# Transposes with the whole array, moved fill matmuls and a new instruction order in a gated-linear-attention and mixer kernel

## The chip, the cores and the metric

The kernel runs on one core of a Trainium2 chip. The metric is the device time of one execution in microseconds (us): the median of several runs. A profile of one more execution gives the trace that is quoted here; its span is a little shorter than the timed runs, since it runs from the first to the last instruction.

## What is computed

First a recurrence over 768 steps for 4 batches and 8 heads of width 48, then a two-layer mixer over tokens and one over channels.

```python
for t in range(S):                                   # S = 768
    state = alpha[:, :, t, :, None] * state + einsum('bhd,bhe->bhde', k[:, :, t], v[:, :, t])
    y[:, :, t] = einsum('bhd,bhde->bhe', q[:, :, t], state)
x = y as [batch 4, token 768, channel 384]
h = maximum(x.T @ w_tok1, 0) @ w_tok2                # 768 -> 256 -> 768, over tokens
u = x + h.T
out = u + maximum(u @ w_ch1, 0) @ w_ch2              # 384 -> 1536 -> 384, over channels
```

## The kernel before

**Attention by blocks.** Each batch is cut into three blocks of 256 steps, so there are twelve blocks, numbered n = 0 to 11. A block's q, k, v and alpha come in four loads (`ld_qt`, `ld_kt`, `ld_vt`, `ld_at`) of 384 KB in float32. In SBUF, partition p holds steps 2p and 2p+1, which the code calls the two values of s (or `sl`); the two halves of the partitions (`hf`) are the two chunks of 128 steps of a block. The steps for one block are:

- `ln`, `cum`: the logarithm of alpha (ACT) and its running sum by matmuls with a triangular matrix; for blocks 0 to 2 (`WIDE`) in the form `lnw`, `cumw`, which spends more TensorE and fewer element-wise passes. `E` and `IE` are the exponentials of plus and minus that sum (ACT).
- `qq`, `kk`: q times E and k times IE, packed in bfloat16 with 64 columns a head (`pkq`, `pkk`); on DVE or POOL. The other blocks have `P`, `k0a` and `q0r` before them. `vb` is v in bfloat16.
- `trq`, `trk`: transposes of `pkq` and `pkk` on TensorE into PSUM; `evq`, `evk`: their copies to SBUF (`tpq`, `tpk`), on ACT or DVE.
- `G0`, `G1`: products of keys and queries; `mask0`, `mask1`: DVE multiplies them by the causal mask and writes `gtm`.
- `K`: the new state's part; `s`, `sa`, `sm`: the state carried on by DVE and POOL.
- `y` (from `gtm` and `vb`), `ia`, a small read called `fe`, `ib` (the inter-chunk part from the state): all in one pair of PSUM banks. `x0`, `x1`: its two halves copied to bfloat16.

**Mixer by batches.** `t1` (tokens 768 to 256) with its relu copies `ht`; `t2` back to 768, added to x in `u`; transposes `up` with copies `ut`; `c1` (24 groups of three matmuls of 384 columns each) with relu copies `rt`; `c2` (six outputs of twelve matmuls), added in `o` and stored by `st`. For batch 0 the matmuls of `t1` are twelve operations of their own, so that each can start when its block's x is there.

**Order.** Nothing is scheduled at run time: `ORDER` is a list of names, each with the letter of its engine (t TensorE, s ACT, v DVE, g POOL, y the load queue on SP), found beforehand by a search. Every engine works through its own names in that order. `Plan.decode` walks the list with a cost model and a due time for every operation; what it decides in the program that runs is which buffer, which PSUM bank or pair of banks each value gets. The transfers of the weights (`ldw_wt1`, `ldw_wt2`, three pieces `ldw_wc1`, two pieces `ldw_wc2`) are issued by POOL, each after the landing of the last load that stands before it in the list. Instructions of DVE and POOL[...] (`kk`, `qq`, `vb`, `sm`, `P`, `k0a`, `q0r`) wait for one another in list order where they change engines.

**Fills.** Before some TensorE steps of blocks 0 to 2 stand three optional operations f0, f1 and f2, which multiply zeros into the bank that the step will overwrite. Those with the letter t are issued, those with n are not. Their purpose is that TensorE keeps busy while its inputs are not there. In the order before, 56 such matmuls of 192 columns are issued, 24 of them ahead of everything else.

**Array modes.** `tr` (64-row transposes), `y`, `ia` and `ib` use the array cut by rows (mode "R" in the planner), `G` and `K` cut by rows and columns ("G"), and all else the whole array. The planner counts 95 ns for a change of mode.

Of the kernel before, what the change touches and what calls it, by code (L numbers as in the profile page):

```python
# [9 lines left out]
BF16 = mybir.dt.bfloat16  # L10
# [53 lines left out]
class Plan:  # L64
# [51 lines left out]
    def decode(self):  # L116
# [14 lines left out]
        for o in self.order:  # L131
# [45 lines left out]
            if e == "PE":  # L177
                a, b = st, st + occ
                while True:
                    w1 = (wi + 1) * 3413.0  # L180
                    if a < w1:
                        d = min(b, w1) - a
                        acc += d
                        a += d
                    if b < w1:
                        break
                    warm = acc > 3000.0 or (warm and acc > 1750.0)
                    wi, acc = wi + 1, 0.0
            if o.dma is not None:
# [6 lines left out]
                else:  # L196
                    s = max(st + lead, dma_in)
                    dma_in = self.landed(s, dur * (1.0 if s < 16000.0 else LATER))
                    o.end = dma_in + tail
# [26 lines left out]
LATER = 1.06  # L226
B, H, S, D = 4, 8, 768, 48
# [10 lines left out]
WIDE = (0, 1, 2)  # L238

# [3 lines left out]
def build(g):  # L243
# [8 lines left out]
    def attention(n):  # L252
# [5 lines left out]
        def O(name, eng, i, **kw):  # L258
            return P.op(f"{name}{n}", eng, pr(i), **kw)

        def fill(nm, bank, sizes=(4, 6, 8)):
            if n >= NB:
                return []
            return [O(f"f{j}{nm}_", {"PE": pe([192] * z)["PE"], "NONE": (0.0, 0.0)}, -100, writes=[bank],
                      emit=lambda e, z=z: g.fill(bank, z)) for j, z in enumerate(sizes)]
# [17 lines left out]
        else:  # L283
# [21 lines left out]
        bk, bq, tpk, tpq = V("pair"), V("pair"), V("tpk"), V("tpq")  # L305
        trk = O("trk", pe([64] * 8), 8, writes=[bk], reads=[pkk], preds=[kk] + fill("trk", bk), emit=lambda e: g.tr(bk, pkk, 2, 1), mode="R")
        trq = O("trq", pe([64] * 8), 8, writes=[bq], reads=[pkq], preds=[qq] + fill("trq", bq), emit=lambda e: g.tr(bq, pkq, 1, 4), mode="R")
        evk = O("evk", either(dve(1024, True), act(1024)), 9, writes=[tpk], reads=[bk], preds=[trk],
                emit=lambda e: g.trev(e, tpk, bk))
        evq = O("evq", either(dve(1024), act(1024)), 9, writes=[tpq], reads=[bq], preds=[trq],  # L310
                emit=lambda e: g.trevq(e, tpq, bq))
        gtm = V("gtm")
        masks = []
        for sl in range(2):
            gp = V("pair")
            G = O(f"G{sl}_", pe([128] * 4), 10 + sl, writes=[gp], reads=[tpk, tpq], preds=[evk, evq] + fill(f"G{sl}", gp),
                  emit=lambda e, sl=sl, gp=gp: g.gmm(gp, tpk, tpq, sl), mode="G")
# [8 lines left out]
        for hf in range(nst):  # L326
# [4 lines left out]
            else:  # L331
# [11 lines left out]
               emit=lambda e: g.inter(yp, tpq, [st and st[0] for st in states[:2]], 0), mode="R")  # L343
        fe = O("fe", either(act(4), dve(4)), 15, reads=[yp], preds=[ia], emit=lambda e: g.fence(e, yp))
        io = O("ib", pe([48] * 4), 15, writes=[yp], reads=[tpq] + [v for v, _ in use], preds=[fe],
               emit=lambda e: g.inter(yp, tpq, [st and st[0] for st in states[:2]], 1), mode="R")
# [104 lines left out]
f1cumw_0n ld_at0y ln0s f2G0_0n f0G0_1n f0y_2n f2trk_0n f2cumw_1t f2trk_1n f0trk_1n f1trk_1n f2G1_0t ld_at1y ln1s  # L451
f2trq_0t f2K_0n f0y_1n f0cumw_0n f2cumw_0n cumw0t E0s IE0s f0G0_2n f0trk_0n f2G1_1n f0cumw_2n f0trk_2n f1cumw_2n
f0K_0n f2G0_1n ld_qt0y qq0v f0cumw_1t f1y_0n f1K_0n f1cumw_1n f1G1_2n cumw1t f2trq_2n f0G1_0t f0y_0n f0trq_0n
f1K_2n f1trq_0n Et0s ld_kt0y f2trq_1n f0K_2n f1trk_0n ld_qt1y f1G1_0n f0trq_1n kk0v f1trq_1n E1s trq0t ld_vt0y
Et1s evq0s ld_kt1y f2y_0n qq1v trk0t trq1t ld_at2y evk0v G1_0t f2G0_2n f2cumw_2n f0G1_2n vb0v ld_vt1y K0t s0_0v
IE1s kk1g evq1s f0G0_0t f2K_2n ld_qt2y mask1_0v f1G0_0t G0_0t trk1t ln2s f0G1_1n cumw2t sa1_0v sm1_0v f1G1_1n
vb1g evk1s f0trq_2n f1G0_1n mask0_0v G0_1t f2y_2n mask0_1v G1_1t y0t ia0t f2y_1n E2s qq2g mask1_1v f0K_1n f1y_2n
IE2s Et2s fe0s ib0t f2K_1n x0_0s x1_0s f1trq_2n ldw_wt10g f1y_1n f2G1_2n f1K_1n K1t f2trk_2t f1trk_2n trq2t
evq2s ld_kt2y kk2v y1t sa0_1v sm0_1g ld_vt2y trk2t evk2v ld_at3y ln13s sa1_1v P3g r13s vb2s G1_2t lnP3s ia1t
mask1_2v ld_qt3y fe1s ldw_wt20g f1G0_2t G0_2t mask0_2v K2t sm1_1g sa0_2v cum3t q0r3g IE3s ib1t x1_1s sm0_2v y2t  # L460
ia2t t1_0_1_0t t1_0_1_1t fe2v ib2t E3s qq3v ld_kt3y t1_0_0_0t k0a3v kk3v x0_1s t1_0_1_2t t1_0_1_3t t1_0_0_1t
x0_2s t1_0_0_2t t1_0_0_3t t1_0_0_4t x1_2s t1_0_0_5t t1_0_1_4t t1_0_1_5t ldw_wc10g trq3t ht_0_0s trk3t evk3v
ht_0_1s t2_0_3t t2_0_1t t2_0_2t t2_0_0t t2_0_4t t2_0_5t u_0_3v u_0_1v u_0_2v ldw_wc12g evq3s G1_3t u_0_0v u_0_4v
u_0_5v ld_at4y P4g lnP4s up_0_1t ut_0_1s up_0_0t G0_3t cum4t E4s ut_0_0v up_0_2t ut_0_2v mask1_3v c1_0_3_0t
rt_0_3_0s ln14s IE4s ldw_wc11g ld_qt4y r14s c1_0_2_0t rt_0_2_0v c1_0_3_1t rt_0_3_1s c1_0_0_0t c1_0_1_1t
rt_0_0_0s ld_at5y q0r4v qq4g P5g ld_vt3y c1_0_2_1t rt_0_2_1s c1_0_9_0t c1_0_8_1t c1_0_1_0t rt_0_1_0s c1_0_10_0t
rt_0_10_0s rt_0_1_1s c1_0_11_1t ldw_wc20g rt_0_11_1v c1_0_11_0t rt_0_11_0s c1_0_9_1t rt_0_9_1s rt_0_9_0s
rt_0_8_1v c1_0_4_0t mask0_3v c1_0_6_1t trq4t evq4s ldw_wc21g lnP5s vb3v rt_0_4_0v c1_0_10_1t c1_0_5_0t rt_0_5_0s
K3t s0_3v sa1_3v rt_0_6_1s c1_0_5_1t rt_0_5_1s ld_kt4y c1_0_4_1t k0a4g kk4v ld_kt5y ln15s cum5t rt_0_10_1s r15s
sm1_3g c1_0_7_0t IE5s y3t ia3t trk4t rt_0_7_0v c1_0_0_1t c1_0_7_1t rt_0_4_1s fe3v ib3t evk4v G0_4t rt_0_0_1s  # L470
G1_4t k0a5g kk5g rt_0_7_1s x1_3v c1_0_6_0t mask0_4v mask1_4v rt_0_6_0v x0_3s c1_0_8_0t ld_qt5y c2_0_2_0t
c2_0_1_0t ld_vt4y E5s rt_0_8_0s c2_0_4_0t c2_0_2_1t c2_0_4_1t c2_0_5_0t c2_0_5_1t q0r5g trk5t qq5v trq5t ld_vt5y
c2_0_1_1t c2_0_5_2t c2_0_1_2t evk5v ld_at6y vb4v K4t sa0_4v sm0_4g evq5s G1_5t mask1_5v ld_kt6y c2_0_4_2t sa1_4v
c2_0_4_3t o_0_4v c2_0_2_2t G0_5t sm1_4v vb5s K5t sa0_5v c2_0_1_3t mask0_5v c2_0_0_0t c2_0_5_3t y4t ia4t fe4v y5t
ld_at7y P6g sm0_5g ia5t ld_qt6y fe5v ib4t x0_4s c2_0_2_3t ib5t x1_4s o_0_1v x0_5v ld_at8y st_0_4y ld_qt7y x1_5v
ld_vt6y P7g lnP7s c2_0_0_1t c2_0_0_2t cum7t ln16s k0a6v ln17s ld_vt9y t1_1_0t r17s r16s lnP6s ld_kt7y st_0_1y
t1_1_1t ht_1_1s o_0_5v ld_vt8y q0r6g ht_1_0v c2_0_3_0t c2_0_0_3t t2_1_1t ld_vt7y st_0_5y t2_1_2t t2_1_0t t2_1_3t
o_0_0v E7s P8g cum6t IE6s IE7s c2_0_3_1t ld_qt9y ln18s u_1_1v t2_1_4t q0r7g qq7g vb6g u_1_0v up_1_0t t2_1_5t
u_1_2v u_1_3v u_1_4v up_1_1t c2_0_3_2t c2_0_3_3t ut_1_0s ut_1_1v c1_1_6_0t rt_1_6_0s c1_1_4_0t u_1_5v c1_1_9_0t
rt_1_9_0s k0a7g up_1_2t ut_1_2s ld_at9y c1_1_0_0t kk7v o_0_2v kk6v rt_1_4_0v c1_1_10_0t rt_1_10_0v E6s c1_1_8_0t  # L480
c1_1_9_1t rt_1_9_1v c1_1_1_0t rt_1_1_0v c1_1_0_1t trk7t evk7v rt_1_8_0s rt_1_0_0s trq7t trk6t evk6v lnP8s
rt_1_0_1s c1_1_6_1t rt_1_6_1v ld_kt8y ld_kt10y evq7s o_0_3v c1_1_11_0t rt_1_11_0v ln19s c1_1_3_0t rt_1_3_0s qq6g
trq6t evq6s K6t s0_6v vb7g K7t cum8t P9g sa1_6v c1_1_2_0t rt_1_2_0v ld_qt8y k0a8g sm1_6g c1_1_7_1t ld_at11y
ld_at10y st_0_2y r18s c1_1_8_1t c1_1_7_0t sa0_7v sm0_7v sa1_7v sm1_7v lnP9s rt_1_7_1v IE8s c1_1_10_1t c1_1_5_0t
rt_1_5_0v E8s G1_6t rt_1_8_1s rt_1_7_0s rt_1_10_1s G0_6t kk8g mask0_6v G0_7t mask0_7v c1_1_5_1t ld_qt11y
ld_vt11y vb8g c2_1_0_0t c2_1_0_1t c2_1_0_2t c1_1_3_1t rt_1_3_1s c1_1_1_1t c2_1_0_3t P10g rt_1_1_1s lnP10s
mask1_6v q0r8g qq8g ln110s G1_7t rt_1_5_1v mask1_7v st_0_0y ld_vt10y K8t sa0_8v cum9t IE9s P11g E9s c2_1_1_0t
c2_1_1_1t c2_1_1_2t y6t ia6t trq8t o_1_0v st_1_0y trk8t r19s fe6s ib6t c1_1_2_1t evk8v x1_6v c2_1_1_3t q0r9v
o_1_1v evq8s c1_1_4_1t G1_8t sm0_8v x0_6s G0_8t c2_1_2_0t c2_1_2_1t qq9g mask1_8v c1_1_11_1t ln111s lnP11s
c2_1_2_2t c2_1_2_3t rt_1_2_1s rt_1_4_1v r111s c2_1_4_0t c2_1_4_1t st_0_3y ld_kt11y mask0_8v y8t ld_kt9y ld_qt10y  # L490
ia8t fe8s rt_1_11_1v y7t ia7t k0a11v trq9t fe7v ib8t ib7t x1_7s c2_1_4_2t c2_1_4_3t x0_7v cum11t vb9g x1_8v
x0_8s t1_2_1t t1_2_0t ht_2_1s c2_1_3_0t c2_1_3_1t o_1_2v ht_2_0s q0r11g st_1_1y t2_2_2t o_1_4v evq9v u_2_2v
t2_2_3t u_2_3v k0a9g E11s t2_2_0t u_2_0v t2_2_5t u_2_5v kk9v c2_1_3_2t t2_2_1t up_2_1t IE11s ut_2_1v u_2_1v
c2_1_3_3t c2_1_5_0t c2_1_5_1t trk9t K9t s0_9v sa1_9v c2_1_5_2t t2_2_4t u_2_4v vb10g kk11g qq11g up_2_0t evk9s
G1_9t G0_9t o_1_3v up_2_2t mask0_9v c2_1_5_3t ut_2_0s c1_2_4_0t rt_2_4_0s r110s cum10t st_1_4y c1_2_11_0t IE10s
ut_2_2v c1_2_9_1t sm1_9g mask1_9v rt_2_11_0v c1_2_2_0t rt_2_9_1v E10s c1_2_6_0t rt_2_6_0s c1_2_5_0t rt_2_5_0v
# [22 lines left out]
class Emit:  # L519
# [118 lines left out]
    def fill(self, bank, count):  # L638
        for _ in range(count):
            self.mm(self.bank(bank)[:, 0:192], self.zs[:, 0:128], self.zs, True, True)  # L640
# [255 lines left out]
```

## Time and profile before

| | before |
|---|---|
| time, median of 3 runs | 173.34 us (173.27 to 174.18) |
| span of the profiled execution | 170.6 us |
| TensorE busy | 162.0 us (95%), 2545 matmuls |
| DVE busy | 111.7 us (65%) |
| ACT busy | 85.4 us (50%) |
| POOL busy | 62.3 us (37%) |
| read from HBM, written to HBM | 25.17 MB, 4.72 MB |

The table is the first part of the profile page with the transfers of its third part. Busy time is the union of the recorded intervals of an engine. Matmuls are pipelined, so a full TensorE row says that one was always under way, not that the array ran at its peak. PE is the page's name for TensorE, PEld for its weight loads. L numbers are lines of the kernel; many operations are recorded at the line of a helper (L636 is `mm`, which issues fills, `cum`, `G`, `K`, `y`, `ia` and `ib`; L697 the transposes of `tr`; L722 and L723 the copies by ACT and by the other engines; L681 `kk` and `qq`; L736 the masks; L809 `t1`; L814 `t2`; L825 `up`; L833 `c1`; L838 `c2`).

### The profile page before, as it was taken

Reading aid. Unit: us, or ns where it says so; the run is one execution under the profiler, and the core shown is the slowest. Engines: PE = TensorE matmul, PEld = TensorE weight load, DVE = VectorE, ACT = ScalarE, POOL = GpSimd, SP = SyncE. Lnnn points to the kernel's source line nnn. Section 1 sums busy time; section 2 is a strip of 40 time slices with the busy share of each in tenths; the row PEclk is TensorE's granted clock in tenths of the full one; section 3 lists DMA queues with packets and bytes.
Section 4 is the critical chain, followed back from the end, with each engine's and each line's share of the span. In section 5 each row is a group of like instructions: output and inputs, shape, how many; then the busy total and the mean of one; then the engine's idle time right before and its main releaser. Section 6 shows DMA issues by size and latency. Waiting matters only on the chain.

```text
span 170.6 us, 5831 instructions
## 1 busy us (share of the span) xinstructions
PE 162.0 (95%) x2545; PEld 104.2 (61%) x2545; DVE 111.7 (65%) x204; ACT 85.4 (50%) x164; POOL 62.3 (37%) x69
## 2 busy tenths in 40 slices
PE   7978599999999999999999999999999999999992
PEld 7656474665566665666656666765666566655660
DVE  4289675684786775889997678867876372613151
ACT  3788573687881345589477050579303214373000
POOL 5025676109390147756692532895010000000000
PEclk9999955899999999999999999999999999999999
DMA  5999999999999679999956810111000100302132
GB/s 140 324 326 266 257 259 266 217 237 268 235 204 262 186 198 328 277 261 245 266 143 191 234 52 0 50 46 50 4 0 4 46 0 6 138 0 92 47 141 93
DMA packets 57226, 27.12 MB, mean 159 GB/s; under 512 B 50416, under 2 KB 57200, under 8 KB 57200
## 3 DMA queue, kind: packets, MB, share of 16 engines
q1 hardware_dynamic: 53376, 23.60, 49.9%
q0 software_dynamic: 3824, 3.15, 12.0%
q8 instruction: 20, 0.33, 0.8%
q14 instruction: 6, 0.05, 0.1%
HBM read 25.17 MB, written 4.72 MB: 175 GB/s over the span
## 4 chain that ended last, share of the span: by engine, by line
PE 85%; SPq 5%; DMA 4%; DVE 2%; POOL 1%; issue 1%; POOLq 0%
PE ps L838 28%; PE ps L833 28%; PE ps L636 12%; PE ps L809 6%; SPq L598 5%; PE ps L814 5%; DMA qt<-in_q_dram 4%; PE ps L697 3%; PE ps L825 3%; DVE gtm L736 1%; POOL pkq L681 1%; DVE tpk L723 0%; DVE o L842 0%; DVE x L723 0%; POOLq L681 0%
## 5 line engine op out<-in xcount | busy, mean ns | idle before, releaser
L838 PE MATMUL ps<-wc,rt 128*128 128x384 bf16 x288 | 52.3, 326 | 0.1
L833 PE MATMUL ps<-ut,wc 128*128 128x384 bf16 x288 | 51.6, 326 | 0.0
L833 PEld LDWEIGHTS <-wc 128*128 128x128 bf16 x288 | 27.0, 98 | 17.5 <-issue 0.2
L838 PEld LDWEIGHTS <-rt 128*128 128x128 bf16 x288 | 26.8, 98 | 17.0 <-DMA wc<-in_moe_w_ch_dram 0.5
L804 ACT ACTIVATE rt<-ps 128x384 bf16<-128x384 f32 x56 | 25.5, 495 | 19.3 <-PE ps L833 18.8
L806 DVE TENSOR_SCALAR rt<-ps 128x384 bf16<-128x384 f32 x40 | 21.5, 553 | 16.9 <-PE ps L833 12.4
L736 DVE TENSOR_TENSOR gtm<-ps,mk 128x1024 bf16<-128x1024 f32 x24 | 28.9, 1218 | 1.6 <-PE ps L636 1.4
L842 DVE TENSOR_TENSOR o<-ps,u 128x384 f32<-128x384 f32 x24 | 13.2, 553 | 12.3 <-PE ps L838 12.3
L681 POOL TENSOR_TENSOR pkq<-qt,E 128x768 bf16<-128x768 f32 x8 | 14.5, 1812 | 14.7 <-DVE qt L677 8.1
L722 ACT COPY tpq<-ps 128x1024 bf16<-128x1024 bf16 x11 | 14.4, 1312 | 6.5 <-PE ps L697 5.9
L681 POOL TENSOR_TENSOR pkk<-kt,IE 128x768 bf16<-128x768 f32 x5 | 9.1, 1814 | 10.6 <-DMA kt<-in_k_dram 8.6
L818 DVE TENSOR_TENSOR u<-ps,x 128x384 bf16<-128x384 f32 x24 | 11.9, 550 | 1.6 <-PE ps L814 1.6
L722 ACT CAST x<-ps 128x384 bf16<-128x384 f32 x16 | 7.1, 484 | 8.6 <-PE ps L636 7.5
L765 POOL TENSOR_TENSOR ss<-tmp,E 128x192 bf16<-128x192 f32 x8 | 4.1, 509 | 19.3 <-DVE tmp L762 17.4
L809 PE MATMUL ps<-x,wt 128*128 128x384 bf16 x48 | 10.7, 375 | 0.0
L723 DVE COPY tpk<-ps 128x1024 bf16<-128x1024 bf16 x9 | 6.1, 690 | 6.6 <-PE ps L697 6.6
L621 POOL TENSOR_TENSOR at<-at 128x384 f32<-128x384 f32 x9 | 9.0, 996 | 3.7 <-DVE ss L765 1.7
L636 PE MATMUL ps<-tpq,tpk 48*64 48x128 bf16 x384 | 9.1, 227 | 1.1 <-DVE tpk L723 0.8
L723 POOL CAST vb<-vt 128x768 bf16<-128x768 f32 x7 | 5.8, 822 | 9.8 <-PE ps L825 6.2
L814 PE MATMUL ps<-ht,wt 128*128 128x384 bf16 x48 | 9.3, 326 | 0.0
L636 PE MATMUL ps<-zs 128*128 128x192 bf16 x56 | 8.2, 317 | 1.1 <-DVE zs L566 1.1
L636 PEld LDWEIGHTS <-tpk 48*64 48x64 bf16 x384 | 6.3, 110 | 4.4 <-issue 2.0
(76 smaller groups left out, 199.6 us busy)
## 6 DMA issues: line engine op xcount, KB each, us to landing
at<-in_alpha_dram SPq DMA_DIRECT2D x12, 384.0 KB, 6.2
qt<-in_q_dram SPq DMA_DIRECT2D x12, 384.0 KB, 5.6
kt<-in_k_dram SPq DMA_DIRECT2D x12, 384.0 KB, 6.0
vt<-in_v_dram SPq DMA_DIRECT2D x12, 384.0 KB, 5.0
out_dram<-o SPq DMA_DIRECT2D x24, 192.0 KB, 2.1
wc<-in_moe_w_ch_dram POOLq DMA_DIRECT2D x3, 384.0 KB, 9.2
wc<-in_moe_w_ch_dram POOLq DMA_DIRECT2D x2, 576.0 KB, 11.0
wt<-in_moe_w_tok_dram POOLq DMA_DIRECT2D x2, 384.0 KB, 6.9
```

Source lines behind the costliest of these rows:

```text
L636: return self.pe.matmul(out, lhsT=lhsT, rhs=rhs, start=start, stop=stop, skip_group_check=True)
L681: self.shared(self.eng[e].tensor_tensor(self.t(dst)[:, :, :, 0:D], self.t(src).rearrange("p h s d -> p s h d"), bass.AP(tensor=f.tensor, o ...
L722: return self.act.copy(d, s)
L736: self.nc.vector.tensor_tensor(self.t(gtm)[:, sl, :, :], self.pair(gp).rearrange("p a (j t) -> p (a j) t", t=128), bass.AP(tensor=m.tensor ...
L804: self.act.activation(d, s, AF.Relu)
L806: self.nc.vector.tensor_scalar_max(d, s, 0.0)
L809: self.pe.matmul(self.bank(bank)[:, 0:HD], lhsT=self.wt1[:, kc, m * 128 : m * 128 + 128], rhs=self.t(x), start=(kc == 0), stop=(kc == NS - 1))
L814: self.pe.matmul(self.bank(bank)[:, 0:HD], lhsT=self.wt2[:, kc, i * 128 : i * 128 + 128], rhs=self.t(hts[kc]), start=(kc == 0), stop=(kc = ...
L818: self.nc.vector.tensor_tensor(self.t(u), self.bank(bank)[:, 0:HD], self.t(x), ALU.add)
L833: self.pe.matmul(self.bank(bank)[:, 0:HD], lhsT=self.wc1[:, kc, mc * 128 : mc * 128 + 128], rhs=self.t(ut)[:, kc, half * 384 : half * 384 ...
L838: self.pe.matmul(self.bank(bank)[:, 0:HD], lhsT=self.t(rts[mc][0])[:, i * 128 : i * 128 + 128], rhs=self.wc2[:, mc, :], start=(mc == 0), s ...
L842: self.nc.vector.tensor_tensor(self.t(o), self.bank(bank)[:, 0:HD], self.t(u), ALU.add)
```

## The change

There are four parts.

1. Blocks 0 to 2 (`FULL`) transpose with the whole array: eight transposes of 128 by 128 into one PSUM bank in place of sixteen of 64 by 64 into two. The evacuations, `G` and the inter-chunk matmuls address the other layout of `tpk` and `tpq`. It is meant to take fewer instructions and one bank fewer.
2. A fill matmul has 384 columns (the 192 zeros read twice) and the three sizes are 1, 2 and 4 of them.
3. The planner counts loads as landing later (`lag`), asks for more busy time to keep the clock (2100 in place of 1750 ns a window) and takes another cost for `evq` on ACT. [...]
4. With these numbers the order was searched anew. All 900 names are the same, but engines, places and the issued fills differ.

```diff
-                    warm = acc > 3000.0 or (warm and acc > 1750.0)
+                    warm = acc > 3000.0 or (warm and acc > 2100.0)
...
-                    o.end = dma_in + tail
+                    o.end = dma_in + tail + (lag(s) if kind == "i" else 0.0)
...
+def lag(s):
+    return 0.0 if s < 12500.0 else 1100.0 if s < 20000.0 else 2000.0 if s < 30000.0 else 3000.0 if s < 58000.0 else 1500.0
...
+FULL = (0, 1, 2)
...
-        def fill(nm, bank, sizes=(4, 6, 8)):
+        def fill(nm, bank, sizes=(1, 2, 4)):
...
-        bk, bq, tpk, tpq = V("pair"), V("pair"), V("tpk"), V("tpq")
-        trk = O("trk", pe([64] * 8), 8, writes=[bk], reads=[pkk], preds=[kk] + fill("trk", bk), emit=lambda e: g.tr(bk, pkk, 2, 1), mode="R")
+        full = n in FULL
+        kind, mode = ("one", None) if full else ("pair", "R")
+        bk, bq, tpk, tpq = V(kind), V(kind), V("tpk"), V("tpq")
+        shape = [128] * 8 if full else [64] * 8
...
-        evq = O("evq", either(dve(1024), act(1024)), 9, writes=[tpq], reads=[bq], preds=[trq],
+        evq = O("evq", either(dve(1024), {"ACT": (1190.0, 1310.0)}), 9, writes=[tpq], reads=[bq], preds=[trq],
...
     def fill(self, bank, count):
+        z = self.zs
+        zz = bass.AP(tensor=z.tensor, offset=z.offset, ap=[list(z.ap[0]), [0, 2], [1, 192]])
         for _ in range(count):
-            self.mm(self.bank(bank)[:, 0:192], self.zs[:, 0:128], self.zs, True, True)
+            self.mm(self.bank(bank)[:, 0:384], self.zs[:, 0:128], zz, True, True)
...
+    def tr(self, bp, v, full, a, b):
         s = self.t(v)
         for c in range(8):
+            at = c // 2 * a + c % 2 * b
+            src = s[:, c % 2, c - c % 2 : c - c % 2 + 2, :]
+            if full:
+                self.pe.transpose(self.bank(bp).bitcast(BF16)[:, at * 128 : at * 128 + 128], src, self.idn)
+                continue
             for hf in range(2):
...
+    def trev(self, e, d, bp, full):
+        if full:
+            self.copy(e, self.t(d), self.bank(bp).bitcast(BF16))
...
+    def keys(self, tpk, full, pr, hf, j, sl):
+        c = ((j * 2 + sl) * 2 + hf if full else (hf * 4 + j) * 2 + sl) * 64
+        return self.t(tpk)[pr, c : c + 64]
```

The two orders as TensorE, POOL and the load queue see their beginning (fills with the number of their matmuls; the names that are not issued are left out):

```
TensorE before: 24 fills of 192, cumw0, 4 fills, cumw1, 4 fills, trq0, trk0, trq1, G1_0, K0, 10 fills, G0_0, trk1,
  cumw2, G0_1, G1_1, y0, ia0, ib0, K1, 8 fills, trq2, y1, trk2, G1_2, ia1, 6 fills, G0_2, K2, cum3, ib1, y2, ia2,
  two of t1, ib2, ten of t1, trq3, trk3, t2
TensorE after: 11 fills of 384, cumw0, cumw1, 1 fill, trq0, trk0, trq1, 1 fill, G1_0, K0, G0_0, trk1, cumw2,
  G1_1, G0_1, y0, ia0, 2 fills, K1, ib0, 5 fills, trq2, 4 fills, trk2, 4 fills, G0_2, y1, ia1, K2, G1_2, cum3,
  three of t1, ib1, y2, ia2, ib2, nine of t1, trq3, trk3, t2
POOL before: kk1, vb1, qq2, ldw_wt1, sm0_1, P3, ldw_wt2, sm1_1, q0r3, ldw_wc1 (two pieces), P4, ldw_wc1 (third)
POOL after: vb0, sm1_0, vb1, ldw_wt1, qq2, P3, ldw_wt2, sm1_1, sm0_2, ldw_wc1 (two pieces), P4, ldw_wc1 (third)
loads before: at0 at1 qt0 kt0 qt1 vt0 kt1 at2 vt1 qt2 kt2 vt2 at3 qt3 kt3 at4 qt4 at5 vt3 kt4 ...
loads after:  at0 at1 kt0 qt0 qt1 vt0 kt1 at2 vt1 qt2 at3 kt2 vt2 qt3 kt3 at4 kt4 qt4 vt3 at5 ...
```

In the order after, `ldw_wt1` waits for the landing of vt1 (before: qt2), and the first two pieces of `ldw_wc1` for that of qt3 (before: kt3).

## The prediction

> **What bounds the kernel now.** I read the page's slices first, for the clock and the transfers.
>
> ```profile
> PE   7978599999999999999999999999999999999992
> PEclk9999955899999999999999999999999999999999
> DMA  5999999999999679999956810111000100302132
> ```
>
> A slice is 4.27 us. From the eighth on TensorE is full; in slices six to eight (21 to 34 us) it shows 9s under a halved clock. Transfers are dense to about 85 us. Next the chain of waits, in order of time.
>
> ```profile
> 16.32 1.82 POOL pkq L681
> ...
> 20.22 0.70 DVE tpk L723
> ...
> 23.57 1.24 DVE gtm L736
> ...
> 24.86 0.46 PE ps L636 x14
> ...
> 26.11 0.76 PE ps L809 x2
> 26.86 0.27 PE ps L636 x8
> 27.13 3.31 PE ps L809 x10
> 30.45 0.83 PE ps L697 x31
> 31.27 2.06 PE ps L814 x12
> ...
> 155.52 11.71 PE ps L838 x72
> ```
>
> To 24.86 the chain is block 2's attention, paced by its loads and by POOL, DVE and ACT. From 26.1 it is TensorE alone: t1, t2 and the channel matmuls, to 167.24; 3.36 us follow (last add and store). 31.27 to 167.24 is 135.97 us without a gap above 0.1 us. So time can be won only before 31.27, or by less TensorE work after it. Third, windows cut at the clock's edges. Half-microsecond windows put the fall at 20.74 and the rise at 30.98, 10.24 us apart. Columns: stretch, length; busy (count) of PE, PEld, DVE, ACT, POOL; clock; transfers.
>
> ```profile
> 0.26:3.67 3.41, 2.58 (x17) 2.44 (x18) 1.76 (x13) 1.28 (x1) 2.30 (x12) 1.00 0.46 118
> 3.67:7.09 3.42, 3.42 (x25) 2.45 (x24) 0.00 (x0) 2.02 (x3) 0.00 (x0) 1.00 1.17 324
> 7.09:10.50 3.41, 2.29 (x56) 1.64 (x56) 2.91 (x4) 3.41 (x7) 0.00 (x0) 1.00 1.17 325
> 17.33:20.74 3.41, 1.88 (x72) 1.42 (x70) 2.26 (x4) 1.73 (x3) 2.25 (x3) 1.00 1.10 273
> 20.74:24.15 3.41, 3.19 (x63) 2.42 (x64) 2.23 (x4) 2.24 (x5) 2.55 (x4) 0.50 1.23 219
> 24.15:27.57 3.42, 3.21 (x65) 1.97 (x64) 2.70 (x6) 2.02 (x6) 1.96 (x3) 0.50 1.17 255
> 27.57:30.98 3.41, 3.41 (x33) 1.67 (x33) 1.04 (x2) 1.45 (x4) 2.04 (x3) 0.50 1.19 280
> ```
>
> 2.29 us busy kept the clock, 1.88 lost it, 3.2 did not bring it back, 3.41 did. The records say 1.00 from the start, but the 24 opening fills of 192 columns take 4.02 us and the four near 8.0 us 0.49: the array is slow until about 7.09.
>
> [...] clock 0.50, and 10.24 us is three windows. [...] I don't count on the wider transposes for warmth. [...] nine L838 matmuls take 1.57 us after tiled work and 1.46 elsewhere, 0.11 a switch. [...] queue q8 moves 0.33 MB in 20 packets, and loads that land 1.2 us apart slip to 2.4 before vt1 (15.06) and vt2 (19.97).
>
> **The change, part by part.**
>
> *Planner numbers* (lag, 2100, evq 1190/1310) issue nothing; through them only buffer numbers change. Cost nothing by themselves.
>
> *Whole-array transposes*, blocks 0 to 2. Sixteen 64x64 transposes, two at a time, become eight of 128 columns. [...] about 0.25 seen between neighbours (54.14 to 54.38). [...] Evacuations keep 1024 elements a partition (0.69 on DVE, 1.01 to 1.31 on ACT), at the same price. One bank instead of two frees PSUM; no row shows TensorE waiting for a bank then, so nothing.
>
> *Fills.* 10,752 columns before and after, moved. At the start 11 x 384 replace 24 x 192: 4224 columns instead of 4608. At 160 ns per 192 cold they end issuing near 4.6, last record 4.8; la is ready at 5.03, cumw0 starts at 5.09. So a hole of 0.3 to 0.5 us opens in the window that warmed the clock. Around block 2's waits there are 4992 columns instead of 2688: 13 x 163 ns = 2.1 us warm. They replace waiting for qq2, kk2 and evk2. In 17.33 to 20.74 I count fills 0.8 + 0.65 + 0.1, transposes 0.9, rest of block 1 0.2: 2.7, over the 2.29 that held. Hence no fall at 20.74.
>
> *Blocks 0 and 1.* kt0 before qt0, kk0 before qq0, evq0 on DVE (no such row there; between its 0.69 for a plain copy and ACT's 1.31; I take 1.22, the row of another 1024-element read of PSUM by DVE), kk1 from POOL (1.82) to DVE (0.95), vb0 from DVE to POOL. G1 of block 0 moves from 10.95 to about 11.55, but DVE's sum stays near: kk1 11.55 to 12.5, two state steps 0.7, four masks at 1.2 end at 17.9, before 17.85. x1_0 on DVE (0.55) ends 18.4, while kk2 still waits for POOL. Cost nothing: DVE's masks hide it, and block 2's loads come later.
>
> *Order to the second mask of block 2.* ldw_wt1 stands before qq2 on POOL: vb1 ends 16.02, issue 1.00 (its row), qq2 1.81: ends 18.87 against 18.13. What queues behind that issue is qq2, and kk2 on DVE[...]: 18.95 to 19.9 against 19.12. trk2 then goes behind four fills (0.65, hidden in kk2) at 20.05; evk2 ends 21.2 against 20.92. G0, then mask0 21.7 to 22.9. at3 lands ahead of kt2 and vt2; with 1.2 us a load [...], kt2 comes at 18.7 to 19.9 and vt2 at 21 to 22.4. K2 waits for vb2 (0.81 on ACT), G1 stands behind K2 on TensorE: G1 ends 23.5, then sa0 0.35 and mask1 1.22 on DVE: 24.8. Before: 24.81. So up to here nothing is won; the late transpose is paid by the faster Gram work.
>
> *From y2 to t2: the gain.* Warm, y2 and ia2 take 0.5 us instead of 1.2, and ib2 no longer stands behind two half-speed t1 matmuls (26.04 to 26.86): after IE3 and the x1 copies on ACT it ends at 25.8 against 27.0. The two x copies (0.86) end 26.8 against 28.04. Five of t1's nine remaining matmuls run while waiting; four follow at 0.163: 27.5 against 30.45. trq3 and trk3 at full clock take 0.5 to 0.8, needing kk3 by 27.8: kt3 landed at 26.0, has the same place among the loads, and the work of k0a3 and kk3 is 1.5. t2 starts at 28.3 against 31.27: **-3.0 us**.
>
> *After t2.* Same matmuls. By walking both orders, mode switches go from 55 to 52: 3 x 0.11 = **-0.3**. wt1 lands 2 us earlier; wc pieces follow at 31.5, 34.0, 36.8 (spacing of before, 2.5 and 2.8), just ahead of the c1 groups that need them (32, 34.2, 37.2). Loads get 3 us less slack; the lag was put in to keep room. I allow **+0.4** (0 to 1.2) for one such wait. Sum: 173.34 - 3.0 - 0.3 + 0.4 = 170.4.
>
> **Rivals.**
>
> *A, warm-up missed.* The hole leaves 2.9 us of real streaming (3.1 by records) of 3.41 in the first full window; 2.58 did not warm, 3.25 did (the same window before, whose fills issue until 4.93 and leave 0.16). [...] Then cumw1, the transposes and G of blocks 0 and 1 run at half speed; they pile up, so TensorE gets dense and warms by 20.7, some 1.7 us behind: 3.0 - 1.7 = 1.3 is left, and 0.3 of switches less 0.3 of waits: 172.0.
>
> *B, transfers take it back.* DMA share is 1.0 to 1.2 to 60 us, and kt3 or a wc piece landing 2 to 3 us late holds trk3, evk3 or c1 in order. For it: two weight pieces now wait only for qt3 and go before kt3. Against: total bytes are the same and t1 to c1 covers them. 3.0 given back: 173.0, no change.
>
> *C, slower.* [...] the clock is lost before block 2's transposes. Then the four fills (1.28) and trk2 (0.86) cost double: trk2 ends 22.1 against 20.2, evk2 some 1.5 later with all behind it at half speed as before; t2 near 32.8: 173.34 + 1.5 - 0.3 = 174.5. [...] Against: fills alone give 1.55 in that window beside small matmuls, and TensorE's idle stretches 17.98 to 20.96 are what the fills close.
>
> *Also possible*: wait-free downstream, 170.0 or a little below; the same case as my forecast.
>
> **How the numbers follow.** Forecast 0.60, A 0.18, B 0.13, C 0.09. The forecast's bounds: hole and landings worth 1 us either way, 169.2 to 171.4. The range runs from 169.0 to 173.2: it leaves out C and a little of each end. Faster by over 0.5% is below 172.47: the forecast, most of A (0.15), a little of B (0.03): 0.78. Same 0.12, mostly B; slower 0.10, C and B's tail.
>
> **What would show it.** Right: clock 1.00 in all slices from 17 to 34 us; y2 near 24.8 as before; t1's last four matmuls at 163 ns spacing, t2 (L814) at 28 to 28.6; then one unbroken TensorE row of about 135.6 us. Wrong: opening transposes at half speed beyond 7.1 us (A); DMA named as releaser for kt, wc or vt after 27 us, or TensorE idle there (B); 0.50 again after 20 us (C). If t2 starts at 28.3 and the end has not moved with it, my reading that TensorE alone sets the later stage is wrong.

## The result, and the profile after

| | before | changed |
|---|---|---|
| time, median | 173.76 us (173.27 to 174.29) | 171.86 us (171.51 to 172.02) |
| ratio | | 0.989, 95% interval 0.985 to 0.993 |
| span of the profiled execution | 170.6 us | 170.3 us |
| TensorE busy, matmuls | 162.0 us, 2545 | 159.3 us, 2469 |

The change takes 1.9 us away, where 2.9 were forecast. The two profiled executions differ by only 0.3 us, because one kernel's time varies from run to run: 161 runs of the kernel before, pooled over the experiments, have a median of 173.45 us, and its trace is of a run of 172.31, one of the quicker ones. The clock differs too: in a second trace of the changed kernel (experiment 7) its edges lie 0.38 us later, it is at half for one stretch of 3.41 us more, from 8.94 us, and the span is 0.6 us longer (170.9 us). A trace therefore shows here where time goes, and medians over many runs show how much. Ratios below leave out runs over 1.5% above a kernel's fastest, so that they come out nearer to 1 than the medians, which are of all runs.

The slices of the changed kernel, to hold against the three rows shown before:

```profile
PE   7667968999999999999999999999999999999992
PEclk9999995699999999999999999999999999999998
DMA  5999999999999599999109907001002020104042
```

The halved clock has not gone: it moved from slices six to eight to slices seven and eight (25.5 to 34 us). The windows of the changed kernel, cut within 0.11 us of the clock's edges (it fell at 25.62 us), with the columns of before:

```profile
5.25:8.66 3.41, 2.11 (x25) 1.26 (x24) 1.57 (x2) 3.15 (x6) 0.00 (x0) 1.00 1.17 324
...
15.49:18.90 3.41, 3.02 (x94) 2.03 (x94) 2.85 (x5) 2.10 (x5) 2.10 (x2) 1.00 1.16 226
18.90:22.31 3.41, 3.17 (x77) 2.01 (x75) 3.06 (x6) 1.65 (x2) 1.00 (x1) 1.00 1.23 291
22.31:25.73 3.42, 1.76 (x52) 1.16 (x49) 1.98 (x3) 2.27 (x6) 2.12 (x4) 0.98 0.96 250
25.73:29.14 3.41, 2.85 (x54) 1.82 (x54) 3.06 (x5) 1.70 (x5) 1.24 (x3) 0.50 1.09 209
29.14:32.55 3.41, 3.41 (x41) 1.85 (x40) 0.86 (x2) 2.33 (x4) 2.71 (x3) 0.51 1.20 227
```

The stage of the moved fills is full: the two windows up to 22.31 hold 3.02 and 3.17 us of TensorE, where the one of before that lost the clock held 1.88. The next window holds only 1.76, and the clock is gone for two windows instead of three. Why that window is thin, the chain of waits of the changed kernel tells:

```profile
13.98 8.84 DMA vt<-in_v_dram
22.82 0.30 issue
23.11 0.76 POOL wt L622
...
23.90 0.53 POOL ss L793
...
24.73 1.23 DVE gtm L764
...
26.00 1.00 PE ps L648 x40
...
27.62 2.99 PE ps L836 x9
30.61 0.97 PE ps L714 x30
31.58 2.50 PE ps L841 x12
...
36.26 9.75 PE ps L860 x60
```

The load of vt2 takes 8.84 us and now begins the chain. `ldw_wt2` on POOL (L622) waits for its landing, `sm1_1` (L793) stands behind it on POOL, then follow a step of the state and the last mask on DVE. TensorE's timeline around it (L648 is `mm`, L836 `t1`, L841 `t2`; in brackets the idle time ahead and its releaser):

```profile
23.72 0.34 PE L648 MATMUL ps<-vb,pkk 64*64 64x48 bf16 x11 [1.38 <-ACT vb L751]
...
26.00 0.82 PE L648 MATMUL ps<-vb,gtm 64*128 64x48 bf16 x32 [0.55 <-DVE gtm L764]
...
27.55 3.06 PE L836 MATMUL ps<-x,wt 128*128 128x384 bf16 x9
...
31.51 0.82 PE L841 MATMUL ps<-ht,wt 128*128 128x384 bf16 x2
```

`K2` stands 1.38 us for `vb2`, so that G1 behind it ends at 24.4, when the path over POOL has also come free. The last mask ends at 25.96, y2 begins at 26.00, and the nine matmuls of `t1` take 3.06 us at half speed. t2 begins at 31.51; before, at 31.2.

### The profile page after: what moved, and what is told of

The parts are those of the page before. It is cut to its first block, busy times and chain, and to the rows that moved or that the text cites. A ratio compares the mean times of both kernels' runs of the same rounds, so it can differ in the third digit from the quotient of the medians.

```text
span 170.3 us, 5679 instructions
## 1 busy us (share of the span) xinstructions
PE 159.3 (94%) x2469; PEld 100.8 (59%) x2469; DVE 116.6 (68%) x207; ACT 83.3 (49%) x158; POOL 62.5 (37%) x72
## 4 chain that ended last, share of the span: by engine, by line
PE 83%; SPq 7%; DMA 5%; DVE 1%; issue 1%; POOL 1%; ACT 0%; ACTq 0%; DVEq 0%
PE ps L865 28%; PE ps L860 28%; PE ps L648 11%; SPq L610 7%; PE ps L836 5%; DMA vt<-in_v_dram 5%; PE ps L841 5%; PE ps L714 3%; PE ps L852 2%; DVE gtm L764 1%; POOL wt L622 0%; DVE o L869 0%; POOL ss L793 0%; ACT junkACT L751 0%; DVE tmp L790 0%
## 5 line engine op out<-in xcount | busy, mean ns | idle before, releaser
L831 ACT ACTIVATE rt<-ps 128x384 bf16<-128x384 f32 x50 | 23.3, 493 | 30.8 <-PE ps L860 30.1
L833 DVE TENSOR_SCALAR rt<-ps 128x384 bf16<-128x384 f32 x46 | 24.1, 551 | 5.3 <-PE ps L860 4.6
L695 POOL TENSOR_TENSOR pkq<-qt,E 128x768 bf16<-128x768 f32 x7 | 12.7, 1817 | 7.4 <-ACT E L673 5.2
L695 POOL TENSOR_TENSOR pkk<-kt,IE 128x768 bf16<-128x768 f32 x6 | 10.9, 1817 | 11.1 <-ACT IE L676 10.9
L751 ACT COPY tpq<-ps 128x1024 bf16<-128x1024 bf16 x9 | 11.8, 1314 | 4.8 <-PE ps L714 3.7
L793 POOL TENSOR_TENSOR ss<-tmp,E 128x192 bf16<-128x192 f32 x14 | 7.2, 512 | 18.4 <-DVE tmp L790 18.4
L633 POOL TENSOR_TENSOR at<-at 128x384 f32<-128x384 f32 x8 | 7.9, 996 | 10.4 <-DVE vb L752 6.1
L836 PE MATMUL ps<-x,wt 128*128 128x384 bf16 x48 | 10.1, 363 | 0.0
L841 PE MATMUL ps<-ht,wt 128*128 128x384 bf16 x48 | 9.6, 337 | 0.0
L648 PE MATMUL ps<-tpq,tpk 48*64 48x128 bf16 x384 | 8.8, 219 | 0.6 <-DVE tpq L752 0.4
L695 DVE TENSOR_TENSOR pkk<-kt,IE 128x768 bf16<-128x768 f32 x6 | 5.7, 954 | 4.8 <-ACT IE L679 3.9
L751 ACT COPY ut<-ps 128x768 bf16<-128x768 bf16 x6 | 4.8, 800 | 8.2 <-PE ps L852 8.2
L648 PE MATMUL ps<-zs 128*128 128x384 bf16 x28 | 7.5, 404 | 1.2 <-DVE zs L578 1.1
L648 PEld LDWEIGHTS <-tpk 48*64 48x64 bf16 x384 | 6.2, 106 | 3.8 <-issue 2.1
```

What stands on the lines that cost most here:

```text
L648: return self.pe.matmul(out, lhsT=lhsT, rhs=rhs, start=start, stop=stop, skip_group_check=True)
L695: self.shared(self.eng[e].tensor_tensor(self.t(dst)[:, :, :, 0:D], self.t(src).rearrange("p h s d -> p s h d"), bass.AP(tensor=f.tensor, o ...
L751: return self.act.copy(d, s)
L831: self.act.activation(d, s, AF.Relu)
L833: self.nc.vector.tensor_scalar_max(d, s, 0.0)
L836: self.pe.matmul(self.bank(bank)[:, 0:HD], lhsT=self.wt1[:, kc, m * 128 : m * 128 + 128], rhs=self.t(x), start=(kc == 0), stop=(kc == NS - 1))
```

## The experiments

There were three groups, each on another chip and beside its own runs of the kernel before (medians 173.56, 174.19 and 172.91 us). "Mean clock" is the granted clock averaged over a whole run, then over runs. One window of 3.41 us at half speed is 0.01 of it (1.7 of some 171 us). For the kernel before it was 0.967, 0.963 and 0.973. Four questions were put: is it the clock, is it the wider transposes, is it the number of instructions, or is it the order?

### 1. Fills ahead of K2

```diff
-... f1K_2n ... f0K_2n ... f2K_2n ... mask0_2v K2t
+... mask0_2v f0K_2t f1K_2t f2K_2t K2t      # in the changed kernel: 7 x 384 columns
```

> Changed kernel with seven more fills of 384 (1.1 us at full clock) ahead of K of block 2, in the hole of 22.3 to 23.7 us. Theory 1 (the forecast gain was lost because vt2 landed at 22.8, TensorE stood still and the clock fell at 25.7): clock 1.00 through 20 to 33 us, y2 still at 26.0, t2 (L841) near 28.9 in place of 31.5, time about 169.5. Theory 2 (transfers set the later stage, a faster TensorE only waits for them): the clock holds but the time stays at 171.9 within 0.5.

Measured: 171.16 us (169.90 to 171.61, 6 runs), ratio 0.988 (0.983 to 0.993), mean clock 0.994. The clock's row of its slices and four lines of TensorE's timeline (L645, L833, L838 are `mm`, `t1`, `t2`):

```profile
PEclk9999999999999999999999999999999999999999
```

```profile
26.09 0.58 PE L645 MATMUL ps<-vb,gtm 64*128 64x48 bf16 x32 [0.54 <-DVE gtm L761]
...
27.26 1.66 PE L833 MATMUL ps<-x,wt 128*128 128x384 bf16 x9
...
30.40 2.12 PE L838 MATMUL ps<-ht,wt 128*128 128x384 bf16 x12 [0.83 <-DMA wt<-in_moe_w_tok_dram]
```

The clock holds and `t1`'s nine matmuls take 1.66 us instead of 3.06. Yet t2 begins only 1.1 us earlier, since it now waits 0.83 us for wt2, issued at 23.21 behind the landing of vt2 and landed at 30.3. That the fills hold the clock is shown, by this trace and by the mean clocks of the six runs, 0.989 to 1.00. The time lies between the two that were expected, and that the version is faster than the changed kernel is not settled: the ratio to before is 0.988, where the change has 0.989.

### 2. The wide transposes alone, and the change without them

```diff
+FULL = (0, 1, 2)      # transposes_only: with tr, trev and gmm of the change; before's order, fills, numbers
-FULL = (0, 1, 2)      # half_tr: the changed kernel
+FULL = ()
```

> Kernel before with only the whole-array transposes (old order, old fills, old planner numbers). Theory 1: no gain, 173.8 within 0.6, clock lost as before near 20.7 and back near 31. Rival (the transposes carry the measured 1.9 us, by fewer instructions or one bank less): 172.

> Changed kernel with the old 64-row transposes in all blocks. Theory 1: 171.9 within 0.6, since the transposes lie beside loads. Rival (the transposes carry the gain): 173.5 or more.

Measured: the transposes alone 171.76 us, ratio 0.993 (0.990 to 0.995), mean clock 0.984 where before has 0.967; the change without them 172.00 us, ratio 0.992 (0.989 to 0.995), mean clock 0.969. So with the order of before, making only the transposes wider keeps 1.7 windows a run from half speed, and the median falls by 1.8 us (by the ratio 0.7%, some 1.3 us). Taken out of the changed kernel they are not missed in a way that these runs show, 0.992 beside 0.989: the gains of the parts overlap. The clock's row of the transposes alone, and of the change without them:

```profile
PEclk9999975999999999999999999999999999999999
```

```profile
PEclk9985899999999999999999999999999999999998
```

The second row has its slow windows early, at 11 to 18 us, with a span of 169.3: in this trace half speed costs nothing visible while TensorE waits for loads and other engines. It costs where TensorE sets the time, from block 2's y on: `t1`'s nine matmuls take 3.06 us at half speed and 1.66 at full (experiment 1).

What goes with a held clock, the windows of all fourteen traces show. They are 3.41 us long and laid from the clock's edges, since half speed lasts 3.41, 6.83 or 10.24 us in these traces. Count for every matmul that starts in a window its columns, times the share of the array that it uses (the timeline prints the tile: `64*128` of 128 rows and 128 columns is one half). Of the 126 windows that begin at full clock between 3.5 and 42 us, the 17 after which the clock fell hold at most 2792 such columns, and the 109 after which it stayed hold at least 3176. Busy time does not part them. Two windows that kept the clock (fills ahead of K2, 3456 columns; experiment 5, 3328) and two that lost it (the forms alone of experiment 7, 2552; before with wide fills, experiment 4, 2792):

```profile
7.65:11.06 3.41, 1.79 (x26) 1.40 (x25) 3.16 (x4) 2.56 (x6) 0.46 (x1) 1.00 1.17 322
11.47:14.88 3.41, 1.99 (x73) 1.72 (x73) 2.58 (x5) 1.68 (x2) 1.81 (x1) 1.00 1.02 263
22.54:25.95 3.41, 2.51 (x79) 1.71 (x79) 2.47 (x6) 2.30 (x7) 2.04 (x3) 1.00 1.24 267
20.47:23.89 3.42, 2.55 (x81) 1.68 (x73) 3.00 (x4) 2.50 (x6) 2.56 (x4) 1.00 1.24 192
```

By this count sixteen transposes of 64 by 64 are 512 columns and eight of 128 by 128 are 1024. Left out of the count, 14 of the 109 windows would fall below the fullest that lost the clock: transposes count here. The count was found in these traces after the fact; no run was forecast with it.

### 3. Fills of before ahead of block 2's transpose and products

```diff
-... kk2v y1t ... ld_vt2y trk2t ... vb2s G1_2t
+... kk2v y1t ... ld_vt2y f0trk_2t f1trk_2t trk2t ... vb2s f0G1_2t f1G1_2t G1_2t   # 20 x 192
```

> Kernel before with 20 more fills of 192 (1.65 us at full clock), ten ahead of trk2 and ten ahead of G1 of block 2, nothing else. Theory 1 (the clock is worth some 3 us between y2 and t2): clock 1.00 from 17 to 33 us, t2 (L814) at 28.5 to 29, time about 171.2. Theory 2 (transfers set the later stage): 173.8 within 0.5 though the clock holds.

Measured: 174.26 us, ratio 1.001 (0.996 to 1.007), although the mean clock rose to 0.976. The clock did not hold as expected: in the trace it is gone from 12.0 to 18.8 and from 29.0 to 32.4 us, so that the two theories were not told apart. TensorE's waits in this trace, which is of the slowest of the 14 runs (175.38 us), the columns being total, times and longest:

```profile
PE ps L633 <- issue: 2.8, 2, 1.8
```

The kernel before has one such wait of 0.77 us, at 18.71. "issue" is a wait for nothing that the profile records. With the transfers dense (DMA share 1.14 from 20 to 30 us) the two waits last 0.99 and 1.79 us, and each ends 1.4 us after a packet of the instruction queue q8 is through (at 20.47 and 27.21 us). That TensorE waits for instructions there was my guess; the trace does not show it. Theory F below puts such waits down to the number of instructions, and the next two experiments change that number.

### 4. Wider fills: fewer instructions for the same columns

```diff
-        def fill(nm, bank, sizes=(4, 6, 8)):     # of 192 columns
+        def fill(nm, bank, sizes=(2, 3, 4)):     # of 384; fill384 from before, fills384 from experiment 3
```

> Kernel before with its fills 384 columns wide and half as many (28 for 56, same columns, 56 TensorE instructions fewer with their weight loads). Theory F [...]: no wait of TensorE put down to issue, time 172.6 to 173.0 against 173.6. Theory W (the whole-array transposes count as activity and hold the clock): no change, 173.6 within 0.4.

> Kernel before with the ten plus ten extra fills of before_fills, all fills 384 wide: more columns than before, fewer instructions than before (38 fills for 56). Theory F: the issue waits of 1.0 and 1.8 us of before_fills are gone, the clock holds as there, time about 171.8. If the extra fills themselves cost the 0.7 us that before_fills lost: about 174.

Measured: 172.52 us, ratio 0.994 (0.989 to 1.000), mean clock 0.971, for before with wide fills, and 173.00 us, ratio 0.995 (0.992 to 0.999), mean clock 0.986, for experiment 3 with them; before beside them has 0.963. The second has 38 fills of 384 columns where experiment 3 has 76 of 192, so the same columns. It stands 1.2 us below its before, where the narrow fills stood 0.7 above theirs, with the waits down to one of 0.83 us. By ratio the two are 0.6% apart with intervals that overlap, and the clock rose by 0.023 here and by 0.009 there, so the instructions are not the only candidate. In the trace of the second t2 begins at 29.75 us, the earliest of all, and waits 0.30 us for wt2. Wider fills alone gained 1.7 us by medians, at the edge of the interval by ratio; the trace still has one "issue" wait of 0.7 us, where theory F expected none.

### 5. Narrower fills: more instructions

```diff
-        def fill(nm, bank, sizes=(4, 6, 8)):     # transposes_only
+        def fill(nm, bank, sizes=(8, 12, 16)):   # of 96 columns: 112 instructions more
```

> transposes_only with its fills 96 columns wide and twice as many (112 for 56, same columns, 112 TensorE instructions more). Theory F: issue waits of TensorE come back, the gain of 1.8 us is lost, 173.3 or more. Theory W: the gain stays, 171.8 within 0.5.

Measured: 173.37 us, ratio 1.001 (0.998 to 1.005), mean clock 0.980. Its waits on the transfers, of TensorE:

```profile
PE ps L833 <- DMA wt<-in_moe_w_tok_dram: 2.2, 1, 2.2
```

112 instructions more take back the whole gain of the transposes, 1.6 us by medians, 0.9% by ratio, with intervals that do not meet. The clock is as far above its before as with the transposes alone, 0.017: so their hold on the clock does not come from fewer instructions. The time is lost by another way than expected: no "issue" wait, but wt1 issued 0.7 us later (18.85 for 18.14) and landed 3.0 us later (27.7 for 24.6), and `t1` waits. So instructions cost time in this stage, here as later loads. Where, the traces show: in all fourteen the first packet of the instruction queue q8 overlaps the first load issue after 4 us that takes 2.0 to 2.5 us, where those ahead of it take 1.1 to 1.4. Here that is the issue of vt1 at 9.19 us (packet at 9.18), in the kernel before kt2's at 11.48 (12.12), with the transposes alone vt2's at 12.71 (13.24). So qt2, kt2 and vt2 are issued about 1 us later here than with the transposes alone. Whether the one delays the other, no trace shows.

### 6. Several repairs at once

```diff
-... ld_vt2y ... ldw_wt20g ...    ... trq3t trk3t t2_0_2t ... up_0_2t
+... vt2 ahead of at3; ldw_wt2 behind qq2; two fills (f0K_2, f1K_2) before K2
+... block 3's logarithm, cum3, qq3, kk3, trq3, trk3, G0_3 and G1_3 behind t2 and two of three up
```

> Changed kernel with three fills before K of block 2, vt2 loaded ahead of at3, ldw_wt2 issued right behind qq2, and block 3's logarithm, transposes and products moved behind t2 and up. Theory (late transfers, vt2 first and then wt2, are what is left of the loss once the clock holds): vt2 lands near 18.8, y2 at 24.7, t2 near 27.5, c1 waits for wc and starts at 33 to 33.5 against 36.2; time 170.0 to 170.6. If loads of batch 1 then become the wait, about 171.2 as with fill_k2.

Measured: 177.75 us, ratio 1.028 (1.021 to 1.035). By the first half vt2 landed at 18.7 instead of 22.8, but the clock still fell, at 26.56 for one window, and t2 began at 30.45, where 27.5 was expected and experiment 1 has 30.40. The second half put block 3's chain in front of `c1` (L857). Of its timeline:

```profile
37.80 0.61 PE L711 MATMUL ps<-idn,pkk 64*128 64x64 bf16 x16 [1.84 <-DVE pkk L692]
...
40.71 1.76 PE L857 MATMUL ps<-ut,wc 128*128 128x384 bf16 x5
```

`trk3` stands 1.84 us for kk3 and c1 behind it begins at 40.71, where it began at 36.09 in the changed kernel. Edits taken together hid what vt2's earlier landing alone is worth; that is left open.

### 7. Order against forms

By then two theories were left. F: the gain is in the forms (fewer instructions, wide transposes), and the order is worth nothing without them. O: the new order has a gain of its own. Each was built without the other, with the changed kernel again beside them.

```diff
-FULL = (0, 1, 2)                  # order_only: the new order with the old transposes
+FULL = ()
-  sizes=(1, 2, 4), 384 columns    # and fills of 192 with the same columns
+  sizes=(2, 4, 8), 192 columns
-  FULL = (), sizes=(4, 6, 8)      # forms_only: before's order with the new forms
+  FULL = (0, 1, 2), sizes=(2, 3, 4), 384 columns
+... f0trk_2t f1trk_2t trk2t ... f0G1_2t f1G1_2t G1_2t    # forms_fills: forms_only and ten fills
```

> Changed kernel with the old instruction forms: 64-row transposes in all blocks and fills of 192 columns in the double number, so that only order, placing of fills and planner numbers are new (152 TensorE instructions more in the start). Theory F [...]: issue waits of TensorE come back, 172.9 to 173.6. Theory O (the order carries the gain by itself): 171.9 within 0.4.

> Kernel before, old order, with whole-array transposes and fills of 384 in half the number: 152 TensorE instructions fewer with nothing else moved. Theory F: no issue waits, 171.3 or less, so that the instruction forms alone bring all that the change brings. Theory O: 172.5 or more.

> forms_only with five more fills of 384 ahead of trk2 and five ahead of G1 of block 2. If the clock is worth what it costs in half-speed windows (some 0.5 us for each 3.4 us window): clock 0.99 or more, 170.8. If the landing of wt2 stands behind it: t2 waits for the transfer, 171.3.

> The changed kernel once more, to be compared with the three others on one chip: 171.9 within 0.5.

| | median, us | ratio (95%) | mean clock |
|---|---|---|---|
| new order, old forms | 171.25 (22 runs) | 0.996 (0.993 to 1.000) | 0.971 |
| old order, new forms | 171.99 (22 runs) | 0.998 (0.995 to 1.001) | 0.987 |
| the same with ten fills | 171.12 (22 runs) | 0.995 (0.992 to 0.998) | 0.995 |
| the changed kernel again | 172.42 (6 runs) | 0.988 (0.978 to 0.998) | 0.98 |
| before, beside these | 172.91 (60 runs) | 1 | 0.973 |

The ratio of the changed kernel again rests on the two quickest of its six runs. F falls, if narrowly: the order gains 1.7 us by medians, 0.4% by ratio, with the old forms and no higher clock. The forms alone, at 171.99, lie between what F (171.3 or less) and O (172.5 or more) expected, and their ratio does not exclude 1. Runs of equal mean clock, of those that the ratios use, separate the two ways. At 0.97 the new order takes 171.23 us (12 runs) and the kernel before 172.36 (8 runs). At 0.99 the old order with new forms takes 171.63 (13 runs) and the kernel before 171.73 (9 runs). This fits forms that gain through the clock and an order that gains beside it. The gains don't add up: together they are worth 1.9 us in one comparison and 0.5 in the other, whose six runs spread from 169.66 to 172.93.

Where the order's gain lies, the traces show in part. From the first matmul of `c1` to the end of the span take:

| order | span less start of c1, us |
|---|---|
| new | 134.2 (changed), 134.4 (again), 134.2 (order alone), 134.4 (fills before K2), 134.9 with a 0.48 wait on wc (change without wide transposes) |
| old | 135.1 (before), 134.9 (transposes alone), 134.9 and 134.9 (experiment 4), 134.9 (forms and fills), 135.1 (experiment 5), 135.7 with a 0.67 "issue" wait (experiment 3), 136.0 with a 0.98 wait on wc (forms alone) |

Less these waits, every trace of the new order has 134.2 to 134.4, every one of the old 134.9 to 135.1, with the same operations of TensorE behind c1's start. Each trace is of one run, that of the order alone of its slowest (173.28 us). Experiment 6 moves work across that start and is not in the table.

With fills in front of block 2's transpose and second products, the clock's row of the new forms in the old order, and TensorE's one wait on a transfer, read:

```profile
PEclk9999999999999999999999999999999999999999
```

```profile
PE ps L838 <- DMA wt<-in_moe_w_tok_dram: 1.1, 1, 1.1
```

This ends as experiment 1 did: with the clock held, wt2 is waited for. It has the lowest median of its group, 0.1 us below the order alone, and its ratio lies wholly below 1; against the changed kernel again, 1.3 us lower, the few runs of that one leave it unsettled.

## Why the prediction was right in direction and off in size

The time fell inside the forecast's range, but of the signs named for a right forecast only the last came in the trace, a TensorE without a wait from t2 on (135.4 us). The clock was at half from 25.6 to 32.4 us, y2 began at 26.00, t1's nine matmuls took 3.06 us and t2 began at 31.51. The direction was right partly by luck: what the runs show of the gain lies in terms that the forecast had at -0.3 or did not count.

- **Warm clock through block 2's products.** Right up to 25.62 us: 1.00 in the window at 20.74, as forecast, with 3.02 and 3.17 us of work where 2.7 had been counted (the 0.9 in it for transposes was an estimate; in the trace `trq2` and `trk2` take 0.46 us each). The yardstick was not sound: 2.29 us of busy time had held, but a window of 2.55 us lost the clock elsewhere (experiment 2).
- **The failed step: "Hence no fall at 20.74", and from it "t2 starts at 28.3 against 31.27: -3.0 us".** The fall came later, because vt2 landed at 22.82, past the forecast's 21 to 22.4. `K2` and `G1_2` queue behind it, and so do `ldw_wt2` and `sm1_1` on POOL, which the forecast had left out: G1 ended at 24.4 (forecast 23.5), the mask at 25.96 (24.8), and no fill stood ahead of `K2` to fill the window. Experiment 1 put one there and the clock held: this is shown. In the two traces the term -3.0 measures +0.3.
- **What the step overlooked.** t2 needs wt2, which landed at 29.3 in the kernel before and 30.0 in the changed one. So 28.3 was out of reach with a warm clock too. In the four traces where the clock held over t1, t2 began at 29.75 to 30.40; three waited 0.3 to 1.1 us for wt2, and in the fourth (the change without wide transposes, 29.96) it had landed just before, at 29.9. The term should have been near -0.8 to -1.5, bounded by the transfer; rival B's mechanism, on the weight it had not named.
- **The late transpose "paid by the faster Gram work".** Not so in the trace: y2 begins at 26.00 and not at the forecast's 24.8, and does so with the clock held as well (26.09). The load sets it.
- **After t2: -0.3 for mode switches, +0.4 for a wait.** Measured -0.6 from t2's start in the two traces (139.4 and 138.8 us to the end), about -0.65 from c1 on in five traces against eight, and no wait of TensorE on a transfer in the changed kernel. The switches from c1 on go from 51 to 48; at 0.11 us each this is half of it, and the rest is not settled.
- **"I don't count on the wider transposes for warmth."** The caution rested on no trace. The measurement decides otherwise for this case: mean clock 0.967 to 0.984 with the wide ones alone, and the count of experiment 2 parts the windows only with the transposes in it.
- **Instructions cost nothing.** The price of an edit was counted in time of its engine. Experiment 5 puts 1.6 us on 112 instructions. Between 76 narrow fills and 38 wide ones of the same columns lie 1.9 us, each beside its own before, of which the clock may have a part.
- **Rivals.** A did not come in the trace: the hole opened, but the window up to 5.14 us still holds 3.07 us by the records, the three matmuls of `cumw0` that begin at 5.19 take 0.65 us, full speed, and 2.11 us of work in the window after it kept the clock. C's loss of the clock came, after the transposes and not before, for two windows instead of three. What made the change faster where the two traces say nearly the same is then the order's shorter stage after c1 (0.65 us, shown), and fewer half-speed windows over many runs (shown in clock and time for the transposes alone, and in clock, 0.987 for 0.973, for all the forms; for the whole only the mean clock of ten runs speaks for it, 0.978 and 0.980, about one window or 0.5 us). Together these are some 1.2 of the 1.9 us; the rest is open.

## What to carry to other kernels

When a gain comes from an engine running faster, write down the landing of every transfer that its next steps need before pricing it: here the weight of the step after the next one capped 3 us at about 1. Here the clock fell after the window behind the repaired ones, which held 1.76 us of work (22.31): look at the emptiest window behind a repair, by columns times share of the array, which parts all 126 windows here, and not by busy time, which does not. Compare medians of many runs, not two traces. Beside dense loads (DMA share 1.0 to 1.2 here) spend few wide instructions rather than many narrow ones for the same work: 112 more cost 1.6 us.

## What the runs showed of the hardware

- The same program takes 171.7 to 176.2 us in the 50 runs beside experiments 1 to 3; of those that the ratios use, the median falls from 173.66 at a mean clock of 0.96 (13 runs) to 172.11 at 0.99 (3 runs), some 0.5 us for each window of half speed.
- Half speed lasts 3.41, 6.83 or 10.24 us in the traces: one, two or three stretches of 3.41 us. Busy time does not say whether a window keeps the clock: 1.79 us kept it and 2.55 us lost it, so that the planner's 1750 and 2100 ns a window are its assumption. Columns times the share of the array do, in all 126 windows of experiment 2: those with at most 2792 lost it, those with at least 3176 kept it.
- Whole-array transposes of 128 by 128 held the clock better than twice as many of 64 by 64 in pairs: mean clock 0.984 for 0.967.
- The first packet of the instruction queue overlaps a load issue of 2.0 to 2.5 us, where those ahead of it take 1.1 to 1.4, in all fourteen traces: at 12.12 us in kt2's issue from 11.48 to 13.83 in the kernel before, at 14.06 in vt2's from 13.98 to 16.40 in the changed one.
- A load can slip far beside a weight in another queue: vt2 took 8.8 to 9.4 us from issue to landing in the five traces where wt1 was issued within 1.2 us after it, and 5.0 to 6.1 in the nine where wt1 followed 2.6 us or more later. The orders of the loads differ too, so that the weight is the cause is not shown.
